# The down projection of a decode block as a row of eight 128-column blocks in two PSUM banks, residual included, stored by four descriptors

## The chip, the cores and the metric

One NeuronCore of a Trainium2 chip runs the kernel as one program. The metric is device time in microseconds (us), the median of the runs of one kernel. Lower is better.

## What is computed

One decode step (one token, D = 1024) of a pre-layernorm block: grouped-query attention over a cache of 65536 keys (32 query heads, 4 key/value heads of 128), then a gated FFN with F = 3584. All tensors in DRAM are bf16.

```python
h  = x + attention(layernorm(x), k_cache, v_cache, wq, wo)
u  = layernorm(h)
h2 = h + (gelu(u @ w_gate) * (u @ w_up)) @ w_down     # w_down: 3584 x 1024, h2: 1 x 1 x 1024
```

With one token every weight and every key and value is used once, so the 173 MB that are read from DRAM are the bulk of the work. The change concerns the last product, the addition of h, and the store of h2.

## The kernel before

**Loads.** Four large SBUF buffers (`chunk`, 32 KB on each of 128 partitions) are filled in turn by DMAs from SP's queue: the query weights, then key and value chunks in turns, the output weights `wo`, the gate weights (two chunks), the up weights (two chunks, the second in pieces of 2, 1 and 1 rows), and the down weights. A load into a buffer waits until TensorE has read what was in it.

**Vectors as columns or as rows.** A vector of 1024 numbers exists in one of two layouts. As columns it fills a tile of 128 partitions by 8 (`h_col`, line 383: the residual h after attention, in float32). As a row, a product comes out on one partition. The kernel makes rows with column tiles of TensorE: a stationary operand of 128x32, in which only column 0 is not zero, is placed at one of four positions (`tile_position=(0, 32*q)`), and its 512 results land on partition 32q of a PSUM bank. Four such products at q = 0 to 3 use different quarters of the array. A row is turned back into columns by `fold_columns` (line 372): ScalarE copies the bank to SBUF, and float32 matmuls with a selection matrix add it into a column tile.

**Attention and the FFN's first half.** Attention ends in `h_col` (line 384). `layernorm_cols` gives the input `hz`. `ffn_in` (line 391) makes the gate vector and the up vector: rows in two banks (line 173), evacuated by VectorE and ScalarE (lines 184 and 186), turned into columns (line 194); the last two input rows of the up product go straight into columns (line 412). `gl` (line 429) holds the gelu of the gate, and line 433 writes `actz`, the product of both, as stationary operands with 31 zero columns beside each.

**The down projection (lines 436 to 466).** `w_down` is loaded in seven blocks t = 0 to 6 of 512 input rows, 1 MB each: each block is four slices `cc` of 128 rows by 1024 columns. Blocks 0 to 3 are one DMA each (line 448), 4 and 5 too (line 460), and block 6 comes in pieces of 2, 1 and 1 slices.

- Blocks 0 to 3 (`t < TW`): each slice is two matmuls of 512 columns (line 452) into the row bank `dw_ps`; after block 3 `fold_columns` adds the row into `d_ps`, a column tile of 128x8 that was set to zero (line 440).
- Blocks 4 to 6: each slice is eight matmuls (line 464), with 128x128 of the weights as the stationary operand and one column of `actz` as the moving one, straight into `d_ps`.

**The end.** VectorE adds `d_ps` and `h_col` into `h2` (line 468, bf16), and two DMAs (line 471) store it, one from SP's queue and one from ScalarE's. Each writes 128 runs of 4 numbers.

**Order.** No order is written out by hand beyond the source. A scheduler of the language orders each engine's instructions by when their inputs are there, so an engine's order in the trace can differ from the source's. PSUM pools: `ps_m` (3 banks, `misc`), `ps_qk` (3 banks) and `ps_acc` (2 banks, which hold the attention's sums until the last head is done).

Of the kernel before, what the change touches and what calls it, by code (L numbers as in the profile page):

```python
# [9 lines left out]
ALU = mybir.AluOpType  # L10
AX = mybir.AxisListType
BF16 = mybir.dt.bfloat16
F32 = mybir.dt.float32
# [4 lines left out]
def kernel(  # L18
# [13 lines left out]
    nc = tc.nc  # L32
    P = 128
    D = A_x.shape[-1]
# [5 lines left out]
    DC = D // P  # L40
# [13 lines left out]
    NB = 512  # L54
    C4 = NB // P
    DS = D // NB
    FT = F // NB
# [5 lines left out]
    small = ctx.enter_context(tc.tile_pool(name="small", bufs=2))  # L63
    chpool = ctx.enter_context(tc.tile_pool(name="chpool", bufs=4))
    ktpool = ctx.enter_context(tc.tile_pool(name="ktpool", bufs=6))
# [5 lines left out]
    ps_acc = ctx.enter_context(tc.tile_pool(name="ps_acc", bufs=2, space=PSUM))  # L71

    def chunk(name):
        return chpool.tile([P, CW], BF16, name=name, tag="ch")

    def misc(shape, dtype, name):
        return ps_m.tile(shape, dtype, name=name, tag="misc")
# [11 lines left out]
    for t in range(DS):  # L89
        w_sb = chunk("wq_sb")  # L90
        wv = w_sb[:].rearrange("p (c n) -> p c n", c=C4)
# [10 lines left out]
    ident_f = const.tile([P, P], F32, name="ident_f")  # L102
# [10 lines left out]
    for jt in range(4):  # L113
        J, t = divmod(jt, 2)
        for i in range(NI):
            nc.gpsimd.tensor_copy(out=esel[:, jt, SQ * i:SQ * (i + 1)],
                                  in_=ident_bf[:, 64 * J + t:64 * J + 64:2])
# [42 lines left out]
    for v in range(XV):  # L160
        nc.tensor.matmul(x_ps[:].rearrange("p (t c) -> p t c", t=DS), lhsT=xsel[:, v, :], rhs=x_in[:, :, v, :],
                         start=(v == 0), stop=(v == XV - 1))
# [13 lines left out]
    def bank_pair(name, n=2):  # L176
        return [ps_qk.tile([P, NB], F32, name=name, tag="qk") for _ in range(n)]
# [26 lines left out]
    for b in range(2):  # L204
        for hh in range(4):
            nc.tensor.matmul(q_ps[:, 16 * b + hh:16 * b + 16:4], lhsT=q_r[:, b, hh * P:(hh + 1) * P], rhs=sel4[:],
                             start=True, stop=True)
# [142 lines left out]
    for dq in range(OQ):  # L350
        nc.tensor.matmul(o2_ps[:], lhsT=osel[:, dq, :], rhs=o_sb[:, dq * Hq:(dq + 1) * Hq],
                         start=(dq == 0), stop=(dq == OQ - 1))
# [8 lines left out]
    for w0 in range(0, Hq, WN):  # L361
        w_sb = chunk("wo_sb")
        wv = w_sb[:, 0:WN * D].rearrange("p (c n) -> p c n", c=WN)
        nc.sync.dma_start(out=wv, in_=wo_v[:, w0:w0 + WN, :])
        for cc in range(WN):
            c = w0 + cc
            for s in range(DS):
                q = 2 * (c % 2) + s
                nc.tensor.matmul(at_ps[32 * q:32 * q + 32, :], lhsT=o2z[:, c, :], rhs=wv[:, cc, s * NB:(s + 1) * NB],  # L369
                                 start=(c < 2), stop=(c >= Hq - 2), tile_position=(0, 32 * q))  # L370

    def fold_columns(dst, ps, name):

        r = ktpool.tile([P, NB], F32, name=name, tag="kt")
        nc.scalar.copy(out=r[:], in_=ps[:])
        for c in range(C4):
            nc.tensor.matmul(dst[:, c:DC:C4], lhsT=r[:, c:NB:C4], rhs=sel2[:], start=False, stop=False,  # L377
                             skip_group_check=True)
# [4 lines left out]
    h_col = const.tile([P, DC], F32, name="h_col")  # L383
# [43 lines left out]
    nc.vector.tensor_scalar(out=hg[:], in0=g_sb[:], scalar1=0.5, scalar2=None, op0=ALU.mult)  # L427
    gl = small.tile([P, FC], F32, name="gl", tag="gl")
    nc.vector.scalar_tensor_tensor(out=gl[:], in0=th[:], scalar=1.0, in1=hg[:], op0=ALU.add, op1=ALU.mult)
    actz = ptpool.tile([P, FC, 32], BF16, name="actz", tag="pt")  # L430
    nc.gpsimd.memset(actz[:], 0.0)
    u_ps = ffn_in(B_w_up, "u_ps", [4, 2, 1, 1], DC - 2)
# [2 lines left out]

    wd_v = B_w_down.rearrange("(t p c) n -> t p c n", p=P, c=C4)
    DN = CW // (C4 * D)
    TW = min(DN, FT - 1)
    d_ps = misc([P, DC], F32, "d_ps")
    nc.vector.memset(d_ps[:], 0.0)  # L440
    dw_ps = bank_pair("dw_ps", 1)[0]
    for t in range(FT):
        if t % DN == 0:
            w_sb = chunk("wd_sb")
        o = (t % DN) * C4 * D
        wv = w_sb[:, o:o + C4 * D].rearrange("p (c n) -> p c n", c=C4)
        if t < TW:
            nc.sync.dma_start(out=wv, in_=wd_v[t])
            for cc in range(C4):
                for s in range(DS):  # L450
                    q = 2 * (cc % 2) + s
                    nc.tensor.matmul(dw_ps[32 * q:32 * q + 32, :], lhsT=actz[:, t * C4 + cc, :],
                                     rhs=wv[:, cc, s * NB:(s + 1) * NB], start=(t == 0 and cc < 2),
                                     stop=(t == TW - 1 and cc >= C4 - 2), tile_position=(0, 32 * q))
            if t == TW - 1:
                fold_columns(d_ps, dw_ps, "dw_r")
            continue
        r0 = 0
        for sz in (2, 1, 1) if t == FT - 1 else (C4,):
            nc.sync.dma_start(out=wv[:, r0:r0 + sz, :], in_=wd_v[t][:, r0:r0 + sz, :])  # L460
            for cc in range(r0, r0 + sz):
                for j in range(DC):
                    k, c = divmod(j, C4)
                    nc.tensor.matmul(d_ps[:, j:j + 1], lhsT=wv[:, cc, k * NB + c:(k + 1) * NB:C4],  # L464
                                     rhs=actz[:, t * C4 + cc, 0:1], start=False, stop=False, skip_group_check=True)
            r0 += sz
    h2 = small.tile([P, DC], BF16, name="h2", tag="h2")
    nc.vector.tensor_tensor(out=h2[:], in0=d_ps[:], in1=h_col[:], op=ALU.add)  # L468
    out_v = out[0, 0].rearrange("(t p c) -> t p c", p=P, c=C4)
    for t in range(DS):  # L470
        (nc.sync if t % 2 == 0 else nc.scalar).dma_start(out=out_v[t], in_=h2[:, t * C4:(t + 1) * C4])


# [28 lines left out]
```

## Time and profile before

| | |
|---|---|
| Device time, median of 3 runs | 414.23 us (414.22 to 414.49) |
| The profiled execution: its own time | 414.39 us |
| Its span in the trace | 412.6 us |
| Read from DRAM | 173.02 MB, 419 GB/s over the span |
| Busy share of the span: TensorE matmuls / VectorE / ScalarE | 60% / 49% / 9% |
| Packets under 512 B / all | 1152 / 7697 |

The page of a profile describes one execution. Its span runs from the program's first instruction to its last; the execution's own time is 1.8 us longer, for what lies around the span. In the rows, "x" counts instructions, the first time behind the bar is the group's busy time in us and the next the mean of one in ns; "idle before" names what ended the engine's wait. PE is TensorE's matmuls and PEld its weight loads, DVE is VectorE, ACT ScalarE, POOL GpSimd, SP the engine whose queue issues the loads. A letter q behind an engine's name means its instruction queue.

### The profile page before, as it was taken

The page shows a single profiled execution, that of the slowest core. Times are in us where ns is not written, and L with a number is a line of the kernel's source. Part 1 is how long each engine was busy: PE and PEld are TensorE (multiplying, and loading weights), DVE is VectorE, ACT ScalarE, POOL GpSimd, SP SyncE. Part 2 cuts the span into 40 slices and gives each one's busy share as a digit, 9 for nine tenths or more (in the row PEclk, how much of TensorE's full clock was granted, in tenths as well). Part 3 has the DMA queues.
Part 4 walks back from the last instruction along what each step waited for, and adds up shares of the span by engine and source line. Part 5 has one row for each costly group of instructions (what it writes and reads, how often), then busy time and mean ns, then how long its engine had stood idle before and what let it go on. Part 6 is the DMA issues. An engine that isn't in the chain of part 4 may idle for free.

```text
span 412.6 us, 3869 instructions
## 1 busy us (share of the span) xinstructions
PE 248.1 (60%) x1583; PEld 113.7 (28%) x1583; DVE 203.2 (49%) x258; ACT 38.3 (9%) x139; POOL 28.2 (7%) x102
## 2 busy tenths in 40 slices
PE   1375777698491838665566388192828335457855
PEld 1142222233130313221222233030314113225524
DVE  2107999999593909766575389293910000011000
ACT  1000000070000080000003400000070000000000
POOL 8205000210000220000000000000000000000000
PEclk9999889969886877895959688777775555667655
DMA  8999999999999999999999999999999999999992
GB/s 356 419 445 422 438 426 436 424 438 426 437 426 438 426 434 429 435 424 435 426 435 430 432 429 435 427 435 429 430 432 432 430 432 432 419 432 418 415 421 108
DMA packets 7697, 173.26 MB, mean 420 GB/s; under 512 B 1152, under 2 KB 1152, under 8 KB 1792
## 3 DMA queue, kind: packets, MB, share of 16 engines
q1 hardware_dynamic: 7488, 173.02, 97.9%
q8 instruction: 12, 0.20, 0.2%
q10 hardware_dynamic: 192, 0.00, 0.0%
q14 instruction: 5, 0.04, 0.0%
HBM read 173.02 MB, written 0.00 MB: 419 GB/s over the span
## 4 chain that ended last, share of the span: by engine, by line
DMA 61%; DVE 21%; issue 9%; PE 8%; SPq 0%; POOLq 0%; ACT 0%; POOL 0%; ACTq 0%
DMA k_sb<-in_A_k_cache_dram 43%; DVE kt L257 17%; DMA wd_sb<-in_B_w_down_dram 9%; DMA v_sb<-in_A_v_cache_dram 8%; PE qk_ps L261 5%; DVE mx L272 2%; DVE sc L271 2%; PE acc_ps L310 1%; PE g_ps_w L173 1%; PE o_ps L324 0%; PE bc_ps L285 0%; SPq L92 0%; POOLq L497 0%; ACT acc_sb L321 0%; PE mxT_ps L279 0%
## 5 line engine op out<-in xcount | busy, mean ns | idle before, releaser
L261 PE MATMUL qk_ps<-kt,qs 128*128 128x512 bf16 x512 | 145.6, 443 | 74.4 <-DVE kt L257 72.7
L257 DVE STREAM_TRANSPOSE kt<-k_sb 128x1024 f32<-128x1024 f32 x128 | 146.2, 1207 | 49.7 <-DMA k_sb<-in_A_k_cache_dram 49.7
L261 PEld LDWEIGHTS <-qs 128*128 128x128 bf16 x512 | 55.6, 109 | 161.3 <-issue 115.2
L294 ACT ACTIVATE pt<-sc,nbias 128x256 bf16<-128x256 f32 x64 | 31.5, 494 | 249.9 <-DVE nbias L287 249.9
L310 PE MATMUL acc_ps<-v_sb,pt 128*32 128x512 bf16 x512 | 36.8, 435 | 14.0 <-DMA v_sb<-in_A_v_cache_dram 14.0
L326 DVE TENSOR_TENSOR oT_all<-o_ps,rl 128x8 bf16<-128x8 f32 x4 | 0.7, 167 | 56.4 <-PE o_ps L324 56.4
L271 DVE STREAM_TRANSPOSE sc<-qk_ps 128x512 f32<-128x512 f32 x32 | 22.1, 692 | 3.3 <-PE qk_ps L261 3.2
L310 PEld LDWEIGHTS <-pt 128*32 128x32 bf16 x512 | 13.7, 106 | 33.1 <-issue 25.0
L272 DVE TENSOR_REDUCE mx<-sc 128x8 f32<-128x512 f32 x32 | 22.0, 688 | 1.1
L324 PE MATMUL o_ps<-sel,acc_sb 128*128 128x8 f32 x32 | 7.5, 364 | 22.5 <-ACT acc_sb L321 22.5
L219 POOL MEMSET qs<- 128x2048 bf16 x4 | 7.2, 1802 | 99.8 <-PE qk_ps L261 99.8
L173 PEld LDWEIGHTS <-xz 128*32 128x32 bf16 x162 | 6.9, 134 | 25.5 <-issue 21.4
L324 PEld LDWEIGHTS o_ps<-sel,acc_sb 128*128 128x128 f32 x32 | 7.1, 327 | 23.6 <-ACT acc_sb L321 23.6
L173 PE MATMUL qw_ps<-wq_sb,xz 128*32 128x512 bf16 x64 | 7.2, 629 | 9.0 <-DMA wq_sb<-in_A_wq_dram 9.0
L223 POOL COPY qs<-qsel 32x32 bf16<-32x32 bf16 x64 | 11.2, 247 | 19.3 <-DVE qsel L214 18.6
L294 ACT ACTIVATION_READ_ACCUMULATOR pt<-sc,nbias 128x1 f32 x64 | 12.0, 188 | 0.0
L369 PE MATMUL at_ps<-wo_sb,o2z 128*32 128x512 bf16 x64 | 6.9, 607 | 8.5 <-DMA wo_sb<-in_A_wo_dram 8.5
L358 POOL MEMSET o2z<- 128x1024 bf16 x1 | 0.9, 950 | 155.9 <-PE acc_ps L310 155.9
L173 PE MATMUL g_ps_w<-wgu_sb,xz 128*32 128x512 bf16 x56 | 6.9, 609 | 4.9 <-DMA wgu_sb<-in_B_w_gate_dram 3.8
L384 DVE TENSOR_TENSOR h_col<-hc_ps,x_col 128x8 f32<-128x8 f32 x1 | 0.2, 167 | 17.9 <-PE hc_ps L377 17.9
L468 DVE TENSOR_TENSOR h<-d_ps,h_col 128x8 bf16<-128x8 f32 x1 | 0.2, 167 | 14.4 <-PE d_ps L464 14.4
L184 DVE COPY q_r<-qw_ps 128x512 f32<-128x512 f32 x1 | 0.7, 692 | 13.2 <-PE qw_ps L173 13.2
(100 smaller groups left out, 102.7 us busy)
## 6 DMA issues: line engine op xcount, KB each, us to landing
k_sb<-in_A_k_cache_dram SPq DMA_DIRECT2D x16, 4096.0 KB, 29.7
v_sb<-in_A_v_cache_dram SPq DMA_DIRECT2D x16, 4096.0 KB, 33.3
wq_sb<-in_A_wq_dram SPq DMA_DIRECT2D x2, 4096.0 KB, 16.9
wo_sb<-in_A_wo_dram SPq DMA_DIRECT2D x2, 4096.0 KB, 33.3
wgu_sb<-in_B_w_gate_dram SPq DMA_DIRECT2D x2, 3584.0 KB, 34.0
wd_sb<-in_B_w_down_dram SPq DMA_DIRECT2D x6, 1024.0 KB, 24.4
wgu_sb<-in_B_w_up_dram SPq DMA_DIRECT2D x1, 3584.0 KB, 31.6
wgu_sb<-in_B_w_up_dram SPq DMA_DIRECT2D x1, 1792.0 KB, 26.5
```

The costliest lines, as they stand in the source:

```text
L173: nc.tensor.matmul(banks[t // 4][32 * q:32 * q + 32, :], lhsT=rows_z[:, ci, :], rhs=w_row[:, t * NB:(t + 1) * NB], start=first, stop=last, ...
L219: nc.gpsimd.memset(qs[:], 0.0)
L223: nc.gpsimd.tensor_copy(out=qs[rows, :, s, SQ * i + s:SQ * (i + 1):NS], in_=qsel[rows, :, g * rep:(g + 1) * rep])
L257: nc.vector.transpose(out=kt[:], in_=k32[:, s * W:(s + 1) * W])
L261: nc.tensor.matmul(qk[:], lhsT=st["qs"][:, jt, s, :], rhs=mv[:, :, J, :, t], start=(s == 0 and jt == 0), stop=(s == NS - 1 and jt == 3))
L271: nc.vector.transpose(out=sc.rearrange("p n h s -> p (n h s)"), in_=qk[:])
L272: nc.vector.tensor_reduce(out=st["mx"][:, :, ci], in_=sc.rearrange("p n h s -> p h n s"), axis=AX.XY, op=ALU.max)
L294: nc.scalar.activation(out=pt[:].rearrange("p c n h s -> p (c n) h s")[:, :, r, :], in_=sc[:].rearrange("p c n h s -> p (c n) h s")[:, :, ...
L310: nc.tensor.matmul(acc[32 * c:32 * c + 32, :], lhsT=pt[:, ci % CPH, n, :, :].rearrange("p h s -> p (h s)"), rhs=v_sb[:, n:CH:NN, :], start ...
L324: nc.tensor.matmul(o_ps[:], lhsT=acc_sb[:, t * Dh:(t + 1) * Dh], rhs=sel[:, t:SQ:NS], start=(t == 0), stop=(t == NS - 1))
L358: nc.gpsimd.memset(o2z[:], 0.0)
L369: nc.tensor.matmul(at_ps[32 * q:32 * q + 32, :], lhsT=o2z[:, c, :], rhs=wv[:, cc, s * NB:(s + 1) * NB], start=(c < 2), stop=(c >= Hq - 2), ...
```

## The change

The down projection is made as a row throughout. The 1024 outputs are cut into eight blocks of 128 columns: block 2q + b lies on partition 32q of bank b, for q = 0 to 3 and b = 0, 1. Both banks come from `ps_acc`.

Ahead of the up product in the source, both banks are set to zero and the residual is put into them: 32 float32 matmuls, each with one column of `h_col` as the stationary operand and 32 columns of an identity matrix as the moving one, writing every fourth column of a block.

All seven blocks of `w_down` then run alike: each slice is eight matmuls of 128 columns with the 128x32 stationary operand from `actz`, at the four column positions for bank 0 and again for bank 1. `fold_columns` on the down projection, the column matmuls and the final addition are gone. The loads are the same DMAs in the same pieces.

At the end VectorE copies bank 0 and ScalarE bank 1 to SBUF as bf16, and one DMA from SP's queue stores partitions 0, 32, 64 and 96, each with 256 numbers (512 bytes).

```diff
     gl = small.tile([P, FC], F32, name="gl", tag="gl")
     nc.vector.scalar_tensor_tensor(out=gl[:], in0=th[:], scalar=1.0, in1=hg[:], op0=ALU.add, op1=ALU.mult)
+
+    OB = D // 8
+    d_ps = [ps_acc.tile([P, NB], F32, name="d_ps", tag="acc") for _ in range(2)]
+    for b in range(2):
+        nc.vector.memset(d_ps[b][:, 0:OB], 0.0)
+        for q in range(4):
+            for c in range(C4):
+                nc.tensor.matmul(d_ps[b][32 * q:32 * q + 1, c:OB:C4], lhsT=h_col[:, (q // 2) * C4 + c:(q // 2) * C4 + c + 1],
+                                 rhs=ident_f[:, 64 * (q % 2) + 32 * b:64 * (q % 2) + 32 * (b + 1)],
+                                 start=False, stop=False, skip_group_check=True, tile_position=(0, 32 * q))
     actz = ptpool.tile([P, FC, 32], BF16, name="actz", tag="pt")
     nc.gpsimd.memset(actz[:], 0.0)
     u_ps = ffn_in(B_w_up, "u_ps", [4, 2, 1, 1], DC - 2)
...
-    TW = min(DN, FT - 1)
-    d_ps = misc([P, DC], F32, "d_ps")
-    nc.vector.memset(d_ps[:], 0.0)
-    dw_ps = bank_pair("dw_ps", 1)[0]
     for t in range(FT):
...
-        if t < TW:
-            nc.sync.dma_start(out=wv, in_=wd_v[t])
-            for cc in range(C4):
-                for s in range(DS):
-                    q = 2 * (cc % 2) + s
-                    nc.tensor.matmul(dw_ps[32 * q:32 * q + 32, :], lhsT=actz[:, t * C4 + cc, :],
-                                     rhs=wv[:, cc, s * NB:(s + 1) * NB], start=(t == 0 and cc < 2),
-                                     stop=(t == TW - 1 and cc >= C4 - 2), tile_position=(0, 32 * q))
-            if t == TW - 1:
-                fold_columns(d_ps, dw_ps, "dw_r")
-            continue
         r0 = 0
         for sz in (2, 1, 1) if t == FT - 1 else (C4,):
             nc.sync.dma_start(out=wv[:, r0:r0 + sz, :], in_=wd_v[t][:, r0:r0 + sz, :])
             for cc in range(r0, r0 + sz):
-                for j in range(DC):
-                    k, c = divmod(j, C4)
-                    nc.tensor.matmul(d_ps[:, j:j + 1], lhsT=wv[:, cc, k * NB + c:(k + 1) * NB:C4],
-                                     rhs=actz[:, t * C4 + cc, 0:1], start=False, stop=False, skip_group_check=True)
+                for b in range(2):
+                    for q in range(4):
+                        nc.tensor.matmul(d_ps[b][32 * q:32 * q + 32, 0:OB], lhsT=actz[:, t * C4 + cc, :],
+                                         rhs=wv[:, cc, (2 * q + b) * OB:(2 * q + b + 1) * OB],
+                                         start=False, stop=False, skip_group_check=True, tile_position=(0, 32 * q))
             r0 += sz
-    h2 = small.tile([P, DC], BF16, name="h2", tag="h2")
-    nc.vector.tensor_tensor(out=h2[:], in0=d_ps[:], in1=h_col[:], op=ALU.add)
-    out_v = out[0, 0].rearrange("(t p c) -> t p c", p=P, c=C4)
-    for t in range(DS):
-        (nc.sync if t % 2 == 0 else nc.scalar).dma_start(out=out_v[t], in_=h2[:, t * C4:(t + 1) * C4])
+    h2 = ktpool.tile([P, 2, OB], BF16, name="h2", tag="kt")
+    nc.vector.tensor_copy(out=h2[:, 0, :], in_=d_ps[0][:, 0:OB])
+    nc.scalar.copy(out=h2[:, 1, :], in_=d_ps[1][:, 0:OB])
+    nc.sync.dma_start(out=out[0, 0].rearrange("(q n) -> q n", q=4), in_=h2[0:P:32].rearrange("q b n -> q (b n)"))
```

## The prediction

> **What bounds the kernel now.** I read the page first, then the chain that ended last, then the timeline from the gate product to the end, the groups by form, and the DMA view with the semaphore updates of the store.
>
> The page:
>
> ```profile
> span 412.6 us, 3869 instructions
> ...
> DMA  8999999999999999999999999999999999999992
> GB/s 356 419 445 422 438 426 436 424 438 426 437 426 438 426 434 429 435 424 435 426 435 430 432 429 435 427 435 429 430 432 432 430 432 432 419 432 418 415 421 108
> ```
>
> All 16 DMA engines are busy until the last of the 40 slices: the kernel waits for DRAM, and work on an engine costs time only where it delays a load or comes after the last one. The end of the chain of waits (start, length, what):
>
> ```profile
> 392.63 14.92 DMA wd_sb<-in_B_w_down_dram
> 407.55 0.05 issue
> 407.60 0.44 PE d_ps L464 x8
> 408.04 0.02 issue
> 408.06 0.17 DVE h L468
> ```
>
> The last weights are there at 407.55; eight matmuls, the addition and the stores follow with nothing beside them. The timeline:
>
> ```profile
> 393.36 0.28 DVE L433 TENSOR_TENSOR actz<-u_ps,gl 128x28 bf16<-128x28 f32 x1 [5.85 <-PE u_ps L412]
> ...
> 393.69 1.05 PE L452 MATMUL dw_ps<-wd_sb,actz 128*32 128x512 bf16 x8 [0.37 <-DVE actz L433]
> ...
> 400.12 1.04 PE L452 MATMUL dw_ps<-wd_sb,actz 128*32 128x512 bf16 x8 [1.44 <-DMA wd_sb<-in_B_w_down_dram]
> ...
> 401.85 2.03 PE L377 MATMUL d_ps<-sel,dw_r 128*128 128x2 f32 x8 [0.69 <-ACT dw_r L375]
> ...
> 408.26 0.35 SPq L471 DMA_DIRECT2D out_dram<-h  x1
> 408.26 0.39 ACTq L471 DMA_DIRECT2D out_dram<-h  x1
> ```
>
> In brackets is the idle time before a row. A block of the down weights arrives every 2.48 us (this row begins at 400.12, that of the block before at 397.64) and its matmuls last 1.05, so PE idles 1.44 before each. The DMA view (last figure: us to landing):
>
> ```profile
> out_dram<-h SPq DMA_DIRECT2D x1, 1.0 KB, 3.2
> out_dram<-h ACTq DMA_DIRECT2D x1, 1.0 KB, 3.3
> ```
>
> So the end is 408.26 + 3.32 = 411.58, and 1.02 more to the span's end. Of the 5.05 us behind the last weights 3.32 are the store: the largest term, and one that the change touches.
>
> **The loads.** They are the same DMAs from the same queue in the same order. The only waits in SP's queue on TensorE near here are for the gate buffers (down blocks issued from 369.27, when line 173 has read the first). The first down block lands 23 us after its issue; a gate product that is some microseconds late leaves the queue full. I cost this at nothing; cover gone, each microsecond beyond those 23 would cost one.
>
> **Residual and memsets.** Two memsets of 128x128 float32 on VectorE: 165 ns each (line 97 has that form). In the trace the engines' order is not the source's: the `d_ps` memset of line 440 ran at 364.79, 29 us ahead of `actz`, which the source puts before it. So the new work can run anywhere from `h_col` (362.01, plus 0.17) to the up product (381.50). Behind it on PE are the layernorm's sums, the gate or the up product.
>
> Its price: four float32 matmuls in `fold_columns` make 8 rows, so 32 make 64. One row's bounds are 33 ns (line 412: 56 in 2.00 with a last one of 0.17) and 237 ns (line 377: (2.03 - 0.37) / 7, with 128 weight columns to load): 2.1 to 15.2 us. The new loads have one weight column; the nearest row is line 279's 128x8 float32 load, 83 ns. I take 83 x 64 = 5.3 us. Cover: PE idles 3.72 us (369.27 to 372.99) and 0.72 and 0.71 before the two up chunks; then `actz` may come later. The new blocks (below) take 0.86 us each, so seven could begin at 401.8 instead of 393.69 and still end at 408.0: 8.1 us. In the source's place the cover is 0.72 + 0.71 + 8.1 = 9.5 us, further forward 13.2. Cost nothing at 5.3; at 237 ns a row up to 5.7.
>
> **The blocks.** Line 452's eight matmuls of 512 columns are two rounds of four that run side by side: 1.05 in all, 0.62 for one (its mean is 618 ns), so rounds are 0.43 apart. Proportional to columns, a round of 128 columns is 0.107 apart. A block of 32 matmuls is then 8 x 0.107 = 0.86, less than 2.48. Bounds: 0.107, and 0.43 if a round has a fixed price (3.4 us a block). Line 464's weight load and matmul pairs, 38 ns each (eight in 0.43 with the last 0.17), say that short instructions do issue at 4 in 0.15, so I take 0.107 and keep 0.15 as the likely worst (1.2 a block). The fold (line 375's copy, 0.59, and 2.03) goes; it lay in a DMA wait and gives nothing.
>
> A page speaks against this: the Trainium skill, "TensorE: Matmul & The Clock Gate", section Back-to-back issue gap, gives some 81 ns for each pair of weight load and 128-column matmul in a stream. By it a block would be an estimated 2.6 us, longer than 2.48, seven would end near 411.8, and the sum would turn into about +2.4 us; but that figure is for whole-array pairs, and line 452's 8 in 1.05 show four tiles side by side.
>
> **The last piece** (eight matmuls): before 0.44. After: 0.107 + one of 128 columns, 0.288 (line 346: a 128x32 operand, 128 columns), together 0.40, so **-0.04** (with 0.15 rounds zero, with 0.43 +0.28).
>
> ```profile
> L346 PE MATMUL oh_ps<-ident_bf,oT_all 128*32 128x128 bf16 x1 | 0.3, 288 | 0.3 <-DVE oT_all L326 0.3
> L214 DVE CAST qsel<-qsel_ps 128x128 bf16<-128x128 f32 x1 | 0.3, 292 | 0.4 <-PE qsel_ps L212 0.4
> L464 PE MATMUL d_ps<-actz,wd_sb 128*128 128x1 bf16 x96 | 3.9, 173 | 0.4 <-DMA wd_sb<-in_B_w_down_dram 0.4
> ```
>
> **The evacuation.** Before: 0.02 + 0.17 + 0.03 to the issue. After: VectorE copies bank 0, the form of line 214, 0.29, begun a round before PE ends. ScalarE copies bank 1 later: between line 425's 226 ns for 28 columns and line 375's 586 for 512, 128 columns are 0.30; it begins 0.05 (line 375) to 0.10 (line 186) after PE, take 0.07; 0.03 to the issue. Together 0.40 for 0.22: **+0.18** (+0.1 to +0.3). SP's store now waits for both engines; nothing is queued behind it but the end. ScalarE's queue loses its store.
>
> **The store.** Issue to first packet is 0.84 us in the trace (408.26 to 409.10), and all packets start within 0.25. The rest is landing: SP's 16 completion counts come in from 409.57 to 411.41, ScalarE's from 409.74 to 411.58. So the same store of 8-byte runs was done in 1.31 us on one DMA engine, 1.8 on the middle one, 3.15 on the last; the trace has no store of 512-byte runs. Bounds: 1.3 and 3.3. I take 1.7, near the middle engine, because four runs on few engines wait for fewer last ones and 256 writes of 8 bytes shrink to four: **-1.6** (-2.0 to 0).
>
> The Trainium skill, "DMA: Bandwidth & Descriptors", section Specifications, names read-modify-write below 512 B, which would explain the spread; its section on the anatomy of one DMA puts the fixed cost at about 2.0 us. No row here shows a full-size store; with 2.0 the sum would be about -1.2.
>
> **Sum.** -0.04 + 0.18 - 1.6 = -1.46 us. The profiled execution is 414.39 (span 412.6 and 1.8 around it), 0.16 above the median; applied to the median, 414.23 - 1.46 = **412.8 us**.
>
> **The rivals.**
>
> - *The landing time is not about run length* (the path to DRAM costs 3.2 us, or the four runs are cut small again). For: both stores landed within 0.1 of each other. Against: the first counts at 1.3. Then -0.04 + 0.18 + 0 = +0.1: 414.4. Chance 0.15.
> - *TensorE's rounds don't shrink* (slower). For: no 128-column round at four positions is in the trace, and each needs its own weight load. From 405.06, when block 5 is there, 16 rounds fit into 2.9 us up to 408.0, so it decides above 0.18 a round; at 0.35 a block is 2.8, seven from 393.69 end at 413.3, +5.3 - 1.5 = +3.8: 418.0. At 0.43: 417.8 and 422.5. Against: line 464's issue rate. Chance 0.08.
> - *The float32 residual lands ahead of the up product at 237 ns a row*: 5.7 - 1.5 = +4.2, 418.4; it decides above 150 ns (9.5 / 64). Chance 0.04.
>
> **How the numbers follow.** My case, a landing under 2.3 us with PE in time, has 0.73. What a measurement can tell from no change is 0.2%, 0.83 us: faster is below 413.4, and my case with a landing of 2.3 sits there. Faster 0.73; same 0.15, the first rival; slower 0.12, the other two. The range takes the landing's lower bound with the evacuation's (414.23 - 2.0 + 0.1 = 412.3) and reaches to the first rival, 414.4; it leaves out the two slow cases and a little more.
>
> **What would show it.** Right: last weights near 407.55 as before, PE waiting for DMA before the down blocks, the last eight matmuls in about 0.4, ScalarE's 128x128 copy at 0.30, one store from SP with about 1.7 to landing, the span near 411.1. Wrong: a landing of 3 or more; down blocks that run back to back with no DMA wait before them; idle time on VectorE or ScalarE beyond 408.1 that ends with PE; residual rows of 0.15 or more between the gate and the up product.

## The result, and the profile after

The changed kernel takes **413.12 us** (412.91 to 413.42, 9 runs), the kernel before, run beside it, 414.22 (413.94 to 414.49, 9 runs): a ratio of 0.9974, 95% interval 0.9965 to 0.9983, so 1.1 us faster by the medians. The prediction was 412.8, with a range of 412.3 to 414.4. The profiled execution took 412.98 us, its span is 410.9. Its page:

```profile
span 410.9 us, 4172 instructions
...
DMA  8999999999999999999999999999999999999994
GB/s 351 415 450 417 447 421 438 426 434 434 429 437 424 440 414 447 418 439 427 428 437 423 440 427 440 423 431 431 432 431 434 431 432 434 427 427 417 416 421 180
```

DRAM still sets the pace up to the last slice. The end of the chain of waits (start, length, what):

```profile
392.45 15.02 DMA wd_sb<-in_B_w_down_dram
407.46 0.04 issue
407.50 0.43 PE d_ps L459 x8
407.93 0.02 issue
407.95 0.27 ACT h L465
```

The last weights are there at 407.46 (before 407.55), eight matmuls last 0.43 (0.44), and the chain leaves through ScalarE's copy, which ends last. Then the store; the timeline, with the idle time before a row in brackets:

```profile
362.29 0.48 PE L437 MATMUL d_ps<-ident_f,h_col 128*1 128x32 f32 x6 [0.26 <-DVE h_col L384]
...
363.21 1.73 PE L437 MATMUL d_ps<-ident_f,h_col 128*1 128x32 f32 x58
...
366.63 3.60 PE L173 MATMUL g_ps_w<-wgu_sb,xz 128*32 128x512 bf16 x28 [1.17 <-DVE xz L156]
372.81 3.60 PE L173 MATMUL g_ps_w<-wgu_sb,xz 128*32 128x512 bf16 x28 [2.57 <-DMA wgu_sb<-in_B_w_gate_dram]
...
399.91 1.04 PE L459 MATMUL d_ps<-wd_sb,actz 128*32 128x128 bf16 x32 [1.43 <-DMA wd_sb<-in_B_w_down_dram]
...
407.50 0.40 PE L459 MATMUL d_ps<-wd_sb,actz 128*32 128x128 bf16 x8 [0.24 <-DMA wd_sb<-in_B_w_down_dram]
407.85 0.29 DVE L464 CAST h<-d_ps 128x128 bf16<-128x128 f32 x1 [14.54 <-PE d_ps L459]
407.95 0.27 ACT L465 CAST h<-d_ps 128x128 bf16<-128x128 f32 x1 [20.62 <-PE d_ps L459]
408.25 0.65 SPq L466 DMA_DIRECT2D out_dram<-h  x1
```

The residual ran directly behind `h_col`, inside the layernorm: 58 rows in 1.73 us. The gate product before:

```profile
365.68 3.55 PE L173 MATMUL g_ps_w<-wgu_sb,xz 128*32 128x512 bf16 x28 [1.16 <-DVE xz L156]
372.99 3.31 PE L173 MATMUL g_ps_w<-wgu_sb,xz 128*32 128x512 bf16 x28 [3.76 <-DMA wgu_sb<-in_B_w_gate_dram]
```

It began at 366.63 instead of 365.68, 0.95 late, and still waited 2.57 us for its second chunk (3.76 before): the delay was swallowed. PE idles before a down block as it did (1.43 us here, 1.44 before). SP's wait for the store (us in total, times, longest us), after and then before:

```profile
SPq L492 <- DMA out_dram<-h: 0.9, 1, 0.9
SPq L497 <- DMA out_dram<-h: 2.9, 1, 2.9
```

The store's four packets of 512 bytes start at 409.49 and its last completion count is in at 409.91: **1.67 us from issue to landing, where it was 3.32**. Step by step up to that landing: last weights -0.09, to the last matmul's end -0.02, evacuation +0.10 (0.32 for 0.22), store -1.65, together -1.67 before rounding.

### The profile page after: what moved, and what is told of

Same layout as the page of the kernel before. It is cut to its first block, busy times and chain, and to the rows that moved or that the text cites. A ratio compares the mean times of both kernels' runs of the same rounds, so it can differ in the third digit from the quotient of the medians.

```text
span 410.9 us, 4172 instructions
## 1 busy us (share of the span) xinstructions
PE 244.9 (60%) x1735; PEld 112.3 (27%) x1735; DVE 203.2 (49%) x259; ACT 37.9 (9%) x139; POOL 28.2 (7%) x102
## 4 chain that ended last, share of the span: by engine, by line
DMA 61%; DVE 21%; issue 9%; PE 8%; ACT 0%; SPq 0%; POOLq 0%; POOL 0%; ACTq 0%
DMA k_sb<-in_A_k_cache_dram 44%; DVE kt L257 18%; DMA wd_sb<-in_B_w_down_dram 9%; DMA v_sb<-in_A_v_cache_dram 8%; PE qk_ps L261 5%; DVE mx L272 2%; DVE sc L271 2%; PE acc_ps L310 1%; PE g_ps_w L173 1%; PE o_ps L324 0%; SPq L92 0%; POOLq L492 0%; ACT acc_sb L321 0%; PE mxT_ps L279 0%; DVE mx L277 0%
## 5 line engine op out<-in xcount | busy, mean ns | idle before, releaser
L310 PEld LDWEIGHTS <-pt 128*32 128x32 bf16 x512 | 13.6, 105 | 33.4 <-issue 25.2
L223 POOL COPY qs<-qsel 32x32 bf16<-32x32 bf16 x64 | 11.2, 247 | 17.8 <-DVE qsel L214 17.1
L459 PE MATMUL d_ps<-wd_sb,actz 128*32 128x128 bf16 x224 | 7.7, 308 | 7.2 <-DMA wd_sb<-in_B_w_down_dram 6.8
```

The costliest lines, as they stand in the source:

```text
L223: nc.gpsimd.tensor_copy(out=qs[rows, :, s, SQ * i + s:SQ * (i + 1):NS], in_=qsel[rows, :, g * rep:(g + 1) * rep])
L310: nc.tensor.matmul(acc[32 * c:32 * c + 32, :], lhsT=pt[:, ci % CPH, n, :, :].rearrange("p h s -> p (h s)"), rhs=v_sb[:, n:CH:NN, :], start ...
L459: nc.tensor.matmul(d_ps[b][32 * q:32 * q + 32, 0:OB], lhsT=actz[:, t * C4 + cc, :], rhs=wv[:, cc, (2 * q + b) * OB:(2 * q + b + 1) * OB], ...
```

## The experiments

E2 edits the kernel before, the other eleven the changed kernel. The diffs are cut to the lines that matter. E1, E3, E10 and E11 change only which bytes the store takes, so what they store is not the product; E8, E9 and E12 change the product's layout too. A "run" of bytes is a stretch that lies together in DRAM and is written as one packet. "Landing" is from the start of the DMA's issue to its last completion count; it and the times of packets are read from the traces' packet and semaphore records. The kernel before took 414.42 us beside E1 to E4, 414.21 beside E5, E6, E8 and E9, 414.11 beside E7, E10 and E11, and 414.43 beside E12; the differences below are to these.

### Is it the store or the row? (E1, E2)

E1: the changed kernel with the stores of before.

```diff
-    nc.sync.dma_start(out=out[0, 0].rearrange("(q n) -> q n", q=4), in_=h2[0:P:32].rearrange("q b n -> q (b n)"))
+    out_v = out[0, 0].rearrange("(t p c) -> t p c", p=P, c=C4)
+    for t in range(DS):   # 2 x 128 runs of 8 bytes, SP and ScalarE
+        (nc.sync if t % 2 == 0 else nc.scalar).dma_start(out=out_v[t], in_=h2[:, t, 0:C4])
```

> The changed kernel with the store of before: two DMAs (SP's queue and ScalarE's), each 128 runs of 8 bytes, read from the first four columns of both halves of h2, so the numbers stored are not the product. Store theory (the gain is the store's shape): issue to landing goes from 1.67 back to 3.2 to 3.3 us, the span grows by about 1.6, the time is 414.2 to 414.8. Row theory (the gain comes from how the product ends or from loads that come earlier): the time stays within 0.3 us of 413.1.

Measured: 414.50 us, ratio 1.0004 (0.9995 to 1.0013). The DMA view:

```profile
out_dram<-h SPq DMA_DIRECT2D x1, 1.0 KB, 2.9
out_dram<-h ACTq DMA_DIRECT2D x1, 1.0 KB, 3.0
```

The landing is back at 3.0 us, a little under the 3.2 that I expected, and the whole gain is gone. The row form alone (down blocks, residual, two copies) gives nothing in the time; the store is the gain.

E2: the kernel before with its two stores as one DMA of 256 runs of 8 bytes on SP's queue.

> The kernel before with one store from SP's queue (128 partitions, two runs of 8 bytes each) for two stores from two queues. Run-length theory: as many 8-byte runs as before, landing 3.2 +- 0.2 us after the issue, time 414.2 +- 0.3. Two-queue theory (the stores hinder each other): landing near 1.8 to 2.3, time 413.2 to 413.7.

Measured: 414.20 us, ratio 0.9997 (0.9989 to 1.0006), landing 3.1. One queue or two is no matter.

### What of the store? (E3, E4, E8, E10, E11)

E3: 16 runs of 128 bytes from partitions 0 to 15.

```diff
-    in_=h2[0:P:32].rearrange("q b n -> q (b n)")
+    in_=h2[0:16, 0, 0:D // 16]
```

> The changed kernel with one store of 16 runs of 128 bytes from partitions 0 to 15 (not the product) for 4 runs of 512 from partitions 0, 32, 64, 96. If only the number of runs and the time to issue count: the issue takes 0.35 instead of 0.65 us, first packet 0.84 instead of 1.24 after it, landing 1.3, time 412.7. If runs below 512 bytes are slow: the landings spread as with 8-byte runs, 2 to 3.2 us after the issue, time 413.4 to 414.7.

Measured: 412.61 us, ratio 0.9959 (0.9946 to 0.9971): faster than the changed kernel's. Timeline and DMA view:

```profile
408.21 0.36 SPq L466 DMA_DIRECT2D out_dram<-h  x1
```

```profile
out_dram<-h SPq DMA_DIRECT2D x1, 2.0 KB, 1.3
```

The issue lasts 0.36 us, where the changed kernel's lasts 0.65, and its first packet starts 0.85 us after the issue began instead of 1.24. It lands after 1.35 us, so runs of 128 bytes do not bring the old landing back. This store reads VectorE's half of `h2` alone: it is issued at 408.21, before ScalarE's copy ends (408.26), which gives it some 0.05 us beside the landing; E11's does the same.

E4: the row stored as 256 runs of 8 bytes out of four partitions (each group of 4 numbers has 4 empty ones behind it in SBUF).

> The changed kernel, same four partitions, but h2 padded in SBUF so that the store is 256 runs of 8 bytes from the four partitions. Run-length theory: the slowest DMA engine of before took 2.2 us for 16 short writes, 0.14 each; 64 on each of four engines are then up to 9 us, landing 5 to 10 us after the issue, time 416.5 to 421.5. Engine theory (the spread of before is the last of 16 engines, whatever the runs): landing 1.7 to 2.2, time 413.1 to 413.6.

Measured: 415.87 us, ratio 1.0036 (1.0023 to 1.0048), landing 4.32. Between its first packet and its last count lie 3.0 us; in E2 the same number of runs from 128 partitions took 2.2. So four partitions are no cure: 256 runs of 8 bytes cost 2 to 3 us wherever they come from. Both expectations missed: by run length alone I had put the landing at 5 to 10 us and the time at 416.5 or more, which is too much, and the theory of the last engine (413.1 to 413.6) is out.

E8: eight blocks on eight partitions (0, 16, ... 112) of one bank, one VectorE copy, eight runs of 256 bytes.

```diff
-    in_=h2[0:P:32].rearrange("q b n -> q (b n)")
+    in_=h2[0:P:16]
```

> The changed kernel with the eight blocks on eight partitions (0, 16, 32 to 112) of one bank: the stationary operand's column that is not zero is column 0 or column 16. One copy by VectorE, one store of eight runs of 256 bytes. Engine-count theory (a store from 16 partitions is issued in 0.36 us with the first packet after 0.85, one from 4 partitions in 0.65 and 1.24, because fewer than 16 DMA engines take part): with 8 the issue is still 0.6 or so, landing 1.6 to 1.7, time 412.9 to 413.3. If the price goes with the number of engines left out: first packet at about 1.1, landing 1.55, time 412.9. If runs under 512 bytes are slow: landing above 2, time above 413.4.

Measured: 413.21 us, ratio 0.9977 (0.9968 to 0.9987); the issue lasts 0.71 us. No better than four partitions. I read this as "fewer than 16 partitions cost", until E9 (below) stored 16 runs of 128 bytes from partitions 0, 8, ... 120 and still took 0.59 us for the issue, 1.24 to the first packet and 1.73 to the landing. E3 has the same 16 runs; only the step between the partitions differs. E10 settles it: the changed kernel's four runs of 512 bytes, from partitions 0 to 3.

```diff
-    in_=h2[0:P:32].rearrange("q b n -> q (b n)")
+    in_=h2[0:4].rearrange("q b n -> q (b n)")
```

> The changed kernel with one difference: its store reads four neighbouring partitions (0 to 3) instead of partitions 0, 32, 64 and 96, so the output is not the product; four runs of 512 bytes as before, waiting on both copies. The store of 16 runs from partitions 0 to 15 was issued in 0.361 us with its first packet 0.854 us after the issue began; that of 16 runs from partitions 0, 8, ... 120 took 0.588 and 1.24 us, like the changed kernel's (0.645 and 1.24). So the number of partitions alone does not order them. Theory A (what costs is the step between the partitions): issue 0.35 to 0.45 us, first packet 0.85 us after it, landing 1.25 to 1.3 us instead of 1.67, time 412.7 us. Theory B (two causes: fewer than 16 partitions, and a step): issue 0.6 to 0.7 us, first packet 1.2 us after, landing 1.65 us, time 413.1 us as the changed kernel.

Measured: 412.59 us, ratio 0.9961 (0.9946 to 0.9976). Timeline:

```profile
408.26 0.35 SPq L466 DMA_DIRECT2D out_dram<-h  x1
```

Issue 0.35 us, first packet after 0.78, landing 1.20 instead of 1.67. Theory A (the step is what costs) holds: **the step between the partitions costs the changed kernel 0.47 us**, all of it ahead of the first packet. Why a step costs is open.

E11: 128 runs of 16 bytes from 128 neighbouring partitions.

```diff
-    in_=h2[0:P:32].rearrange("q b n -> q (b n)")
+    in_=h2[:, 0, 0:D // P]
```

> The changed kernel with a store of 128 runs of 16 bytes from 128 neighbouring partitions (not the product). From first packet to last count, 256 runs of 8 bytes took 2.18 us (one queue) and 3.0 us (from four partitions), 16 runs of 128 bytes 0.49 us, 4 runs of 512 bytes 0.43 us. If the cost goes with the number of writes (8.5 us per thousand, above a floor of about 0.4): 128 x 0.0085 = 1.1 us plus up to 0.4, so 1.1 to 1.5 us, landing 1.95 to 2.35 us. If every run below some length costs the same whole penalty whatever their number: 2.2 us, landing 3.0 us. If the cost goes only with bytes: 0.45 us, landing 1.3 us.

Measured: one run, 412.68 us; from first packet to last count 0.57 us, landing 1.4. My price for each short write fell: 128 writes should have cost 1.1 us or more. Of the three cases in the expectation, the last (only the bytes count) is nearest. E12 below has the same store in another kernel, over 11 runs, with the same 0.57 and 1.41. Between 256 runs of 8 bytes and 128 runs of 16 lie 1.6 us, between those and four runs of 512 bytes 0.14. Whether it is the length (8 or 16) or the number (256 or 128) that turns it isn't told apart: every store of 8-byte runs here has 256 of them.

The Trainium skill, "DMA: Bandwidth & Descriptors", section Specifications, puts the boundary at 512 B, below which a write is read, modified and written. These stores show no cliff there: with neighbouring partitions runs of 512, 128 and 16 bytes land after 1.20, 1.35 and 1.41 us. The page's fixed 2.0 us for one DMA (section on the anatomy of one DMA) is a fit for DMAs issued from GpSimd, which no run here has; the landings of these stores from SP's queue, for runs of 16 bytes and more, are below it (1.20 to 1.73).

### Does TensorE have the room that the prediction gave it? (E5, E6, E7, E9)

E5 issues each slice's eight matmuls twice, the second time with a stationary operand of zeros; E6 three times.

```diff
+                for rp in range(2):            # E6: range(3)
...
+                    lhsT=actz[:, t * C4 + cc, :] if rp == 0 else zrow[:],
```

> The changed kernel with the eight matmuls of each slice made twice, the second time with a stationary operand of zeros. Parallel-tiles theory (a round of four is 0.107 apart): a block is 16 rounds, 1.9 us, below the 2.48 between blocks, so PE still waits for the loads, and only the last piece grows, by two rounds, 0.2 us: the span is 0.2 longer. Rival (a round has a price near 0.2 or more that was just covered): blocks of 3.2 us or more, the span 5 us longer or more. Outside the span: if the share of the time that lies outside it (2.0 us in the changed kernel, 1.8 in the one before) follows the number of TensorE instructions (1735 and 1583), it is 2.3 here with 1959; if not, 2.0.

> As the run before, with the eight matmuls three times (two of them with zeros). Parallel-tiles theory: a block is 24 rounds, 2.57 us, just above the 2.48 between blocks, so PE becomes the bound from the first down block at 393.4: 28 slices of 0.64 end near 411.5 instead of 407.9, span 414.5, 3.6 longer than the changed kernel's. Outside the span: 2.6 us if it follows the number of TensorE instructions (2183), 2.0 if not.

Measured: E5 414.74 us, ratio 1.0012 (1.0003 to 1.0022); E6 420.94, ratio 1.016 (1.0145 to 1.0176). Expected were spans 0.2 and 3.6 us longer than the changed kernel's; the medians grow by 1.6 and 7.8. E5's runs spread from 413.95 to 415.43, and the profiled one is the slowest. It isn't the rounds: a part of E5's timeline, and its waits.

```profile
396.11 0.43 PE L462 MATMUL d_ps<-wd_sb,zrow 128*32 128x128 bf16 x8
396.33 0.42 PE L462 MATMUL d_ps<-wd_sb,actz 128*32 128x128 bf16 x6
397.97 0.29 PE L462 MATMUL d_ps<-wd_sb,actz 128*32 128x128 bf16 x2 [1.23 <-issue]
...
404.17 0.23 PE L462 MATMUL d_ps<-wd_sb,actz 128*32 128x128 bf16 x2 [2.47 <-issue]
...
404.52 0.33 PE L462 MATMUL d_ps<-wd_sb,actz 128*32 128x128 bf16 x8
404.63 0.33 PE L462 MATMUL d_ps<-wd_sb,zrow 128*32 128x128 bf16 x8
...
408.17 0.29 PE L462 MATMUL d_ps<-wd_sb,actz 128*32 128x128 bf16 x2 [1.30 <-issue]
```

```profile
PE d_ps L462 <- issue: 5.0, 3, 2.5
```

Eight matmuls begin 0.22 us after the eight before them (396.11 to 396.33): 0.11 a round, as predicted. That is the price at a granted clock of 0.50, which the trace shows up to 396.5 in E5 and over the whole down projection of the changed kernel. Behind the 2.47 us stop the clock is 1.00 from 404.1 to 405.1, and the eights are 0.11 apart (404.52 to 404.63): half of that, 0.055 a round.

But PE stops in the middle of a slice with nothing to wait for, and from one stop to the next lie 256 instructions (weight loads and matmuls). In the trace's instruction queue a packet of 16384 bytes, 64 for each of 256 instructions, begins at 395.46, 401.60 and 405.87 and takes 1.1 us; PE goes on 1.2 to 1.5 us after each has ended (397.97, 404.17, 408.17). The packets are TensorE's: each trace has as many of them as its PE instructions fill (12 for 12.4 times 256 in the kernel before, 13 for 13.6 in the changed one, 15 for 15.3 in E5, 17 for 17.1 in E6). So TensorE runs out of code: these blocks of 256 begin 6.1 and 4.3 us apart while the weights come in. E6 has four such stops, 7.7 us in all. The changed kernel uses 64 instructions for each 2.48 us of weights, so 256 in 9.9, and shows no such stop. That the stops are the code's arrival is read from their places and these packets; no run changes the code's loading alone.

E9 is E8 with 16 blocks of 64 columns on 16 partitions, so 448 down matmuls for 224.

```diff
-    JB = 2    # blocks on each of four partition groups
+    JB = 4
```

> As the run before with 16 blocks of 64 columns on 16 partitions (every eighth), 16 matmuls a slice, one copy of 128x64 by VectorE, one store of 16 runs of 128 bytes. Store as in the run with 16 runs of 128 bytes: issue 0.36, landing 1.35. The last piece: four rounds of 64 columns, 0.4 if a round shrinks with its columns, 0.55 if a round cannot be shorter than 0.1; the copy 0.23 for 0.27. The span is then 0.2 to 0.4 shorter than the changed kernel's. Against that, 224 more matmuls: if the share outside the span follows TensorE's instructions, 0.3 more there. Time 412.5 to 413.1.

Measured: 416.35 us, ratio 1.0056 (1.0043 to 1.0068), where I expected 412.5 to 413.1: I had left the code out. Its waits:

```profile
PE d_ps L470 <- issue: 8.7, 3, 4.2
```

E7 issues the residual's matmuls four times as often, three of four with zeros.

> The changed kernel with the residual's 64 f32 matmuls issued four times as often: each of the 64 followed by three with a right side of zeros, so that the values stay. At the 26 ns that one took, 192 more are 5.0 us of TensorE directly behind LN2's column, ahead of the gate product. The gate product of the changed kernel waits 2.6 us for its next weights in its first chunk and takes 3.5 us of TensorE per 9.6 us of arriving weights, so it should catch up within that chunk: time 413.1 us (412.8 to 413.5), with the gate product's start about 5 us later. If the residual's place in the chain matters (TensorE never catches up, or the weight buffers come free later): up to 418 us. A third way, from the runs with more matmuls: more TensorE code ahead of the down product shifts the blocks in which the code arrives; then waits with no releaser appear in the gate or down product, and the time grows by 0.5 to 2 us.

Measured: 413.74 us, ratio 0.9988 (0.9978 to 0.9997), above the 412.8 to 413.5 of the first case that I expected. Its waits, and the gate product's start in its timeline:

```profile
PE d_ps L442 <- issue: 1.9, 1, 1.9
```

```profile
374.70 0.40 PE L175 MATMUL g_ps_w<-wgu_sb,xz 128*32 128x512 bf16 x3
```

The gate product starts 8.1 us later (374.70 for 366.63), a code stop included, and the copies at the end 0.60 later (408.45 for 407.85). Of these 0.60, 0.29 were there before the residual (the output product's last matmuls start at 356.00 for 355.71). By the medians E7 gains 0.37 us where the change gains 1.10. So of 8.1 us some 0.7 show in the medians, and some 0.3 in the trace: nearly all is swallowed, though not all as I expected, and the third way that the expectation named was there as well.

### A version out of both (E12)

> A third version, from what the stores showed: 128 runs of 16 bytes from 128 neighbouring partitions landed 1.41 us after the issue began, 4 runs of 512 bytes from partitions 32 apart 1.67 us, 256 runs of 8 bytes 2.9 to 3.3 us. So the down product stays in columns, as before the change, but each partition holds eight neighbouring elements of the output (128x8, column j of the weights taken with a step of 8) instead of two groups of four; one store of 128 runs of 16 bytes goes from neighbouring partitions on one queue. All 28 slices are done as columns (8 matmuls each, no wide rows and no fold); the residual is in PSUM, put there by four f32 matmuls behind h_col; one VectorE copy evacuates. By the stores: the span of before, 412.55 us, less 3.32, plus 1.41 gives 410.65; with the 1.8 us outside the span that the kernels ending in columns have, 412.45 us, faster than the changed kernel by 0.6 us; with the 2.0 us of the kernels ending in rows, 412.65. If the 16-byte runs landed fast only because of something else in that kernel: landing 2.5 to 3 us, time 413.5 to 414.2. If a step of 8 in the weights slows the weight loads (about 31 ns for each of the pairs at a step of 4): the last piece takes more than 0.43 us, and the time grows by that.

```diff
-    lhsT=wv[:, cc, k * NB + c:(k + 1) * NB:C4]     # step 4, 128x8 in two groups of four
+    lhsT=wv[:, cc, j:D:DC]                         # step 8, eight neighbours on a partition
...
+    nc.sync.dma_start(out=out[0, 0].rearrange("(p j) -> p j", p=P), in_=h2[:])
```

Measured: 413.57 us, ratio 0.998 (0.9971 to 0.9989): better than before, not than the change, and 0.9 to 1.1 us above the two times that I worked out. The store does what it should; the DMA view:

```profile
out_dram<-h SPq DMA_DIRECT2D x1, 2.0 KB, 1.4
```

The weights don't, as the expectation's last case had it. The end of PE in its timeline, its weight loads, and those of the kernel before (groups by form: busy us, mean ns of one | idle before):

```profile
402.55 2.10 PE L456 MATMUL d_ps<-actz,wd_sb 128*128 128x1 bf16 x32 [0.39 <-DMA wd_sb<-in_B_w_down_dram]
405.06 4.01 PE L456 MATMUL d_ps<-actz,wd_sb 128*128 128x1 bf16 x64 [0.40 <-DMA wd_sb<-in_B_w_down_dram]
```

```profile
L456 PEld LDWEIGHTS <-wd_sb 128*128 128x128 bf16 x224 | 13.9, 167 | 1.8 <-DMA wd_sb<-in_B_w_down_dram 1.4 <-issue 0.4
```

```profile
L464 PEld LDWEIGHTS <-wd_sb 128*128 128x128 bf16 x96 | 3.8, 120 | 0.6 <-DMA wd_sb<-in_B_w_down_dram 0.6
```

A load at a step of 8 (16 bytes) lasts 167 ns for 120 at a step of 4, and the pairs of load and matmul come 60 ns apart for 33, both at a granted clock of 0.50. The last 64 run without a pause until 409.07, 1.1 us behind the changed kernel's last matmul. The Trainium skill, "SBUF — State Buffer", section "Door 1: The DMA port swizzle", tells of 16-byte lines that want two hits each for full bandwidth: that fits a step of 16 bytes as slower than one of 8; no run here shows whether 8 is still at full bandwidth. The page's next sentence gives 8 bf16 as free, which these loads contradict if it means the step.

## Why the prediction was right

- **The store** (-1.6, landing 1.7): -1.65, landing 1.67. That the store would give the gain was right; that its size held is luck, for two errors cancelled. I took 0.84 us from issue to first packet from the trace of before; four partitions 32 apart took 1.24. And I took 0.86 for the rest, near the middle engine's time; it was 0.43. The reason, many 8-byte writes, is borne out by E1, E2 and E4, though not whether their length or their number counts. That long runs are needed is not: E11's 16 bytes would have done.
- **The first rival** (the landing is not about run length, 414.4) is out: the new store lands after 1.67 us, and with the old store in E1 the time is the old one. The two stores of before, on whose closeness it leaned, landed 3.15 and 3.32 us after their issue, 0.16 apart and not within 0.1.
- **Evacuation** (+0.18): +0.10. ScalarE's copy, put at 0.30, took 0.27 and began 0.02 behind the end of PE where I had 0.07. The wait for both engines is there: SP's issue follows ScalarE's copy.
- **The last piece** (-0.04): 0.40 in the timeline as worked out, -0.01 to -0.02 in the chain.
- **TensorE's rounds** (0.107): confirmed by E5, 0.11 at a granted clock of 0.50, so the second rival, which needed 0.18, is out. A round is four pairs of weight load and matmul, so a pair takes 27 ns and not the 81 that stood against the prediction; that the four tiles side by side make the difference was argued there and is not shown by a run. What limits more matmuls is a thing that I had not priced, by the reading above the arrival of code; the change stays below it.
- **The residual** (64 rows at 83 ns, 5.3 us, hidden): hidden, but mis-sized. 58 rows in 1.73 us with a tail of 0.24 are 26 ns a row, 1.7 us in all; the third rival, at 237 ns, is out. It ran in the place furthest forward of those that I allowed. E7 shows that more would have been swallowed there.
- **The loads** (nothing): the last weights came 0.09 earlier, within what the runs of one kernel differ by.
- **What the sum left out:** what lies around the span. For the kernel before it is 1.73 to 1.93 us (68 runs beside the experiments), for the changed kernel 1.97 to 2.09 (9 runs), so some 0.2 of the gain is lost there. The steps above are those of the two profiled executions: span -1.66, time -1.41 (412.98 for 414.39). By the medians it is -1.10, because the profiled execution of before was 0.17 above its median and that of the changed kernel 0.14 below. The sum, -1.46, thus forecast 0.3 to 0.4 us too much for the medians. E1 and E8 have the 2.0 too, and E12 has 1.74 to 1.93, so it goes with the row form and not with the store. It isn't the amount of TensorE code: E6, with two more copies of every down matmul, has 2.04 to 2.05. What it is stays open.

## What to carry to other kernels

A last store with nothing behind it is paid from its issue to its landing, so shape it by what the chip shows: here runs of 16 bytes or more from neighbouring partitions land in 1.2 to 1.4 us, a step between the partitions adds 0.38 (E9 against E3) to 0.47 (the changed kernel against E10), and 256 runs of 8 bytes take about 3. Shape it without changing what reads the operands ahead of it: E12 won 1.9 us in the store against the kernel before and lost 1.0 of it in weight loads with too wide a step. Before splitting matmuls into more and smaller ones, count instructions against the time that their data take to arrive: counted from the program's start, the stops of E5, E6, E7 and E9 that end with "issue" all lie multiples of 256 instructions apart, which I read as missing code.

## What was not expected of the hardware

- The step between the source partitions lengthens a store's issue from SP's queue: 0.59 to 0.71 us (steps of 8, 16 and 32) against 0.35 to 0.41 (neighbours), and the first packet comes 1.24 to 1.31 us after the issue began against 0.78 to 0.92.
- From first packet to last count: 256 runs of 8 bytes 2.2 to 3.0 us, 128 of 16 bytes 0.57, 16 of 128 bytes 0.49, 4 of 512 bytes 0.43.
- In E5 blocks of 256 instructions for TensorE came 6.1, 4.3 and 3.4 us apart, and it stopped for 1.2 to 2.5 us when it needed them faster.
- A round of four 128-column matmuls took 0.107 us at a granted clock of 0.50 and 0.055 at 1.00; the 1.00 was granted for the first 1 us behind a stop of 2.47 us (E5).
- Weight loads with a step of 16 bytes took 60 ns a pair against 33 with a step of 8 bytes.
